# Attention and a feed-forward block in one kernel: twelve weight loads put behind small attention loads in the DMA queue

## The chip, the cores and the metric

The kernel runs on one core of a Trainium2 chip. The metric is the device time of one execution in microseconds (us), as the median of several runs. The core's engines are TensorE (PE in the profile, with its weight loads as PEld), VectorE (DVE), ScalarE (ACT), GpSimd (POOL) and SyncE (SP). SP computes nothing here; it issues nearly all DMAs, one after the other, in one queue.

## The reference

Attention without a score matrix, on 8 batches of 8 heads with 576 tokens and head width 64, and then a feed-forward block with a squared ReLU on the 4608 tokens of width 512, hidden width 2048. All data is float32.

```python
def _attn_ref(q, k, v):
    q_s = np.exp(q - np.max(q, axis=-1, keepdims=True))
    q_s = q_s / (np.sum(q_s, axis=-1, keepdims=True) + 1e-09)
    k_s = np.exp(k - np.max(k, axis=2, keepdims=True))
    k_s = k_s / (np.sum(k_s, axis=2, keepdims=True) + 1e-09)
    kv = np.einsum('bhsd,bhse->bhde', k_s, v)
    return np.einsum('bhsd,bhde->bhse', q_s, kv)

def _moe_ref(x, w_in, w_out):
    r = np.maximum(x @ w_in, 0.0)
    return (r * r) @ w_out
```

## The kernel before

**Feed-forward.** The 4608 tokens are taken in nine blocks of 512: eight blocks with the first 512 tokens of each batch, and a ninth with the 64 left over from each. A block has 16 steps, one for each 128 columns of the hidden width. A step has two halves on TensorE: h (lines 406 to 408, twelve products of 128x512 that multiply `wi[fc]` with the attention's output) and o (lines 440 to 442, twelve products that multiply the squared ReLU with `wo[fc]` and add up in four banks). Float32 precision comes from pairs: x, g and the weights are each kept as a high and a low part, and each product is made three times (high with high, low with high, high with low). The o half of a step runs two steps behind its h half (`LAG`).

**Weights.** The 16 pieces of `w_in` (i0 to i15) and the 16 of `w_out` (o0 to o15), 512 KB each, are loaded once, by `load_w` (lines 147 and 149), as raw tiles that stay in SBUF. In the first block each piece is split once into its high and low part by `split_weight`: ScalarE does lines 164 and 166, VectorE lines 168 and 169 (the two halves of a split on VectorE), ScalarE makes the high part (line 176) and GpSimd the low part (line 177). The scratch bank `bank3` is shared by all splits, so line 166 of the next one waits for line 169 of the one before. `load_more(n)` loads the o piece of step n and the i piece of step n + 4; step n of the first block splits the i piece of step n + 4 and the o piece of step n + 2.

**Attention.** A batch has four pairs of heads. For a pair, VectorE takes the maximum of k (`m`, line 218) and of q (`qm`, line 260); for the second batch TensorE transposes m (line 222) and spreads it (line 250); VectorE subtracts it from k (`ke`, line 255), ScalarE takes the exponential, TensorE multiplies with v (line 299), and VectorE scales the result (`rs`, `kvn`, lines 307 to 315). TensorE then transposes q and multiplies (lines 347 to 358) and the result is stored as high and low parts `x_hi`, `x_lo` (lines 188, 189). The first batch is done at the start. While the feed-forward of one batch runs, the attention of the next one is put in between its steps, by the table `slots`. The k, q and v tiles of the second and later batches have two buffers (`NB`), so pairs 0 and 2 use kt0, qt0 and vt0, and pairs 1 and 3 use kt1, qt1 and vt1. A pair's loads are called for when the pair two before it has reached a given unit (`us[i]`, line 538).

**What sets the order.** The program is written as a sequence, and a scheduler with a simulated timeline orders each engine's instructions from it, with priorities (`tc.high_priority`) and with explicit bounds (`tc.issue_after`). On the chip each engine then runs its list in that order. SP's list works with eight completion semaphores in turn: an issue waits for the landing of the load that was issued eight places earlier, and for the engine that last read the buffer. Behind the second batch's first two pairs, lines 519 to 522 call for all weights that are still missing:

```python
    for pr in range(NB):
        load_pair(1, pr)
    for n in range(AHEAD, NFC):
        load_more(n)
```

With `AHEAD = 4` that is twelve o pieces and eight i pieces. The loads of the second batch's third and fourth pairs (pairs 2 and 3) are called for later, from line 538.

Of the kernel before, what the change touches and what calls it, by code (L numbers as in the profile page):

```python
# [17 lines left out]
HALF = 64  # L18
LOW = 5
HIGH = 4  # L20
# [5 lines left out]
EARLY_SPLITS = [("o",2),("o",3),("i",4),("o",0)]  # L26
OFFSET = 100
AHEAD = 4
EARLY = 8
PRE = 4  # L30
LOADS = "k0 q0 v0 k1 q1 v1 k2 q2 w0 v2 k3 q3 v3 w1 w2 w3".split()
# [11 lines left out]
def attention_ffn_kernel(ctx: ExitStack, tc: tile.TileContext, q, k, v, w_in, w_out, out):  # L43
    nc = tc.nc

    B, H, S, D = q.shape
    DM, DF = w_in.shape
    NPAIR = H // 2
    NCC = DM // P
    NFC = DF // P  # L50
# [19 lines left out]
    NB = 2  # L70
# [46 lines left out]
    def load(dst, src, b, pr, n):  # L117
        s = src[b, 2 * pr : 2 * pr + 2]
        lo = s[:, :SPLIT, :].rearrange("h (p j) d -> p h j d", j=LOW)
        hi = s[:, SPLIT:, :].rearrange("h (p j) d -> p h j d", j=HIGH)  # L120
        if n < 2 or b == 0:
            e = nc.scalar if (b, pr, n) in ACT_LOADS else nc.sync
            e.dma_start(dst[:HALF], lo)  # L123
            e.dma_start(dst[HALF:, :, :HIGH, :], hi)
        else:
            for h in range(2):
                nc.sync.dma_start(dst[:HALF, h, :, :D], lo[:, h])
                nc.sync.dma_start(dst[HALF:, h, :HIGH, :D], hi[:, h])

    def tiles(b, pr):  # L130
        i = pr if b == 0 else pr % NB
# [5 lines left out]
    def load_pair(b, pr):  # L137
        for n in range(3):
            load_one(b, pr, n)

    chunks, last = [], []

    def load_w(part, fc):
        raw = stay.tile([P, 512, 2], U32, name=f"raw_{part}{fc}", tag=f"{part}{fc}")
# [333 lines left out]
    us = [attention(0, pr) for pr in range(NPAIR)]  # L478
# [3 lines left out]
    for c in LOADS:  # L482
        i = int(c[1])
# [6 lines left out]
    def load_more(n):  # L490
        load_w("o", order0[n])
        if n + PRE < NFC:
            load_w("i", order0[n + PRE])
# [24 lines left out]

    for pr in range(NB):
        load_pair(1, pr)  # L520
    for n in range(AHEAD, NFC):
        load_more(n)
    steps = [(0, fc) for fc in order0] + [(blk, fc) for blk in range(1, B + 1) for fc in range(NFC)]
    LAG = 2
# [3 lines left out]
    for b in range(1, B):  # L528
        for pr in range(NPAIR):
            if b == 1:  # L530
                base, offs = FIRST_KV + EARLY_STEP * pr, EARLY_AT
            else:
                base, offs = 2 * NFC * (b - 1) + 1 + STEADY_STEP * pr, STEADY_AT
            us = attention(b, pr)
            nxt = b * NPAIR + pr + NB
            if nxt < B * NPAIR:
                i = 5 if b == 1 else 4
                us[i] = lambda f=us[i], nxt=nxt: (f(), load_pair(nxt // NPAIR, nxt % NPAIR))
            for u, o in zip(us, offs):
                slots.setdefault(base + o, []).append(u)  # L540
    for cc, u in enumerate(left_units()):
        slots.setdefault(2 * NFC * (B - 1) + 4 + 6 * cc, []).append(u)


    def in_slot(i):
        for u in slots.get(i, []):
# [60 lines left out]
```

## Time and profile before

| | us |
|---|---|
| median of 3 runs | 905.96 (905.91 to 908.08) |
| the profiled execution | 906.89 |
| its span, first to last instruction | 905.0 |
| TensorE busy in the span | 875.9 |
| VectorE busy in the span | 580.8 |
| ScalarE busy in the span | 408.1 |
| GpSimd busy in the span | 202.1 |

The span is what the trace shows; the profiled execution's own time is 1.89 us longer, and that execution took 0.93 us more than the median of the runs. The mean granted clock of TensorE over the span is 0.993 of full speed. Busy time is a sum over very different stretches: the attention of the first batch and the splitting of the weights fill the first 150 us or so, and from there on the feed-forward products dominate.

### The profile page before, as it was taken

The numbers are of one execution on the slowest core, as the hardware profiler recorded it, in microseconds if no ns is written. First come the engines' busy times: TensorE is split into PE (matmuls) and PEld (weight loads), VectorE is DVE, ScalarE is ACT, GpSimd is POOL, SyncE is SP. The second block draws the span as 40 slices with busy tenths as digits, with TensorE's granted clock in tenths as the row PEclk, the third lists the DMA queues.
The fourth block names the chain that finished last, engine by engine and source line by source line (L and its number), as shares of the span: only waits on it lengthen the run. The fifth ranks groups of instructions, "written<-read, shape, count | busy, mean of one in ns | idle before, by whom it ended". The sixth has DMA issues, their size and how long they took to land.

```text
span 905.0 us, 12673 instructions
## 1 busy us (share of the span) xinstructions
PE 875.9 (97%) x4368; PEld 702.4 (78%) x4368; DVE 580.8 (64%) x1177; ACT 408.1 (45%) x801; POOL 202.1 (22%) x177
## 2 busy tenths in 40 slices
PE   4898989999999999999999999999999999999997
PEld 3576767888878888888888888888888888888885
DVE  6767887887778776878688768876764342222222
ACT  3766756545445443454454444444444232222222
POOL 3666635222213210222122212222222000000000
PEclk9989999999999999999999999999999999999999
DMA  9898211422142223322322123222311030002001
GB/s 234 274 324 246 62 35 54 114 77 82 46 117 71 78 64 89 97 72 71 86 80 81 54 76 96 76 65 65 97 31 32 3 93 1 1 1 46 1 1 46
DMA packets 95743, 73.18 MB, mean 81 GB/s; under 512 B 47552, under 2 KB 85440, under 8 KB 95680
## 3 DMA queue, kind: packets, MB, share of 16 engines
q1 hardware_dynamic: 94944, 71.53, 28.7%
q10 hardware_dynamic: 736, 0.85, 0.4%
q8 instruction: 34, 0.56, 0.2%
q14 instruction: 29, 0.24, 0.1%
HBM read 54.00 MB, written 18.35 MB: 80 GB/s over the span
## 4 chain that ended last, share of the span: by engine, by line
PE 85%; DMA 7%; DVE 4%; SPq 2%; issue 1%; ACT 0%; DVEq 0%
PE bank L406 14%; PE o_ps L440 14%; PE bank L407 14%; PE bank L408 14%; PE o_ps L441 14%; PE o_ps L442 13%; DMA qt<-in_q_dram 4%; DMA raw_i<-in_moe_w_in_dram 3%; PE bank L299 2%; PE bank L378 1%; DMA kt<-in_k_dram 1%; DVE w L169 1%; SPq L149 1%; DVE m L237 1%; SPq L123 0%
## 5 line engine op out<-in xcount | busy, mean ns | idle before, releaser
L406 PE MATMUL bank<-x_hi,wi 128*128 128x512 f32 x568 | 227.6, 401 | 4.3 <-ACT x_hi L188 2.2
L440 PE MATMUL o_ps<-wo,g_hi 128*128 128x512 f32 x576 | 227.5, 397 | 0.8 <-ACT g_hi L419 0.8
L441 PE MATMUL o_ps<-wo,g_hi 128*128 128x512 f32 x576 | 225.7, 392 | 0.0
L407 PE MATMUL bank<-x_lo,wi 128*128 128x512 f32 x568 | 225.6, 397 | 0.0
L408 PE MATMUL bank<-x_hi,wi 128*128 128x512 f32 x568 | 225.2, 396 | 0.0
L442 PE MATMUL o_ps<-wo,g_lo 128*128 128x512 f32 x576 | 224.1, 391 | 0.0
L418 DVE TENSOR_TENSOR r<-r 128x512 f32<-128x512 f32 x128 | 112.0, 875 | 123.3 <-ACT r L412 123.0
L423 DVE TENSOR_TENSOR g_lo<-r,g_hi 128x512 fp32r<-128x512 f32 x132 | 99.3, 752 | 105.8 <-ACT g_hi L419 104.1
L419 ACT CAST g_hi<-r 128x512 fp32r<-128x512 f32 x144 | 89.2, 620 | 129.1 <-PE o_ps L441 77.2
L412 ACT ACTIVATE r<-bank 128x512 f32<-128x512 f32 x142 | 84.5, 596 | 106.1 <-PE bank L408 103.4
L406 PEld LDWEIGHTS bank<-x_hi,wi 128*128 128x128 f32 x568 | 107.6, 190 | 30.9 <-ACT x_hi L188 3.6
L440 PEld LDWEIGHTS o_ps<-wo,g_hi 128*128 128x128 f32 x576 | 108.1, 188 | 25.7 <-ACT g_hi L419 1.0
L408 PEld LDWEIGHTS bank<-x_hi,wi 128*128 128x128 f32 x568 | 107.7, 190 | 24.3
L442 PEld LDWEIGHTS o_ps<-wo,g_lo 128*128 128x128 f32 x576 | 108.1, 188 | 22.9
L441 PEld LDWEIGHTS o_ps<-wo,g_hi 128*128 128x128 f32 x576 | 108.1, 188 | 22.9 <-POOL wo L177 0.2
L407 PEld LDWEIGHTS bank<-x_lo,wi 128*128 128x128 f32 x568 | 107.5, 189 | 22.8 <-issue 0.2
L389 POOL TENSOR_TENSOR x_lo<-xf,x_hi 128x256 fp32r<-128x256 f32 x48 | 39.5, 823 | 378.2 <-ACT x_hi L388 377.4
L332 POOL TENSOR_TENSOR qs<-qT,qs 64x640 fp32r<-64x640 f32 x48 | 81.7, 1703 | 58.7 <-ACT qs L331 50.9
L218 DVE TENSOR_REDUCE m<-kt 128x128 f32<-128x640 f32 x32 | 41.4, 1296 | 18.3 <-DMA kt<-in_k_dram 18.3
L331 ACT CAST qs<-qT 64x640 fp32r<-64x640 f32 x48 | 34.8, 726 | 37.9 <-DMA qT<-bounce 37.4
L380 ACT COPY xf<-bank 64x320 f32<-64x320 f32 (+1 forms) x96 | 37.9, 395 | 22.5 <-PE bank L378 14.3
L265 ACT ACTIVATE qn<-qn 128x640 f32<-128x640 f32 x32 | 23.6, 739 | 53.8 <-DVE qn L262 44.9
(118 smaller groups left out, 775.8 us busy)
## 6 DMA issues: line engine op xcount, KB each, us to landing
out_dram<-o SPq DMA_DIRECT2D x70, 128.0 KB, 2.4
raw_i<-in_moe_w_in_dram SPq DMA_DIRECT2D x16, 512.0 KB, 9.3
raw_o<-in_moe_w_out_dram SPq DMA_DIRECT2D x16, 512.0 KB, 9.0
bounce<-tb SPq DMA_DIRECT2D x24, 320.0 KB, 2.2
qT<-bounce SPq DMA_DIRECT2D x96, 80.0 KB, 2.3
kt<-in_k_dram SPq DMA_DIRECT2D x32, 160.0 KB, 3.0
qt<-in_q_dram SPq DMA_DIRECT2D x30, 160.0 KB, 3.0
vt<-in_v_dram SPq DMA_DIRECT2D x56, 80.0 KB, 2.5
```

The lines of the kernel that those rows point to most:

```text
L218: nc.vector.tensor_reduce(m, kk.rearrange("p h j d -> p h d j"), axis=AX.X, op=ALU.max)
L332: nc.gpsimd.tensor_tensor(qs[other], qT[own], qs[own].bitcast(F32), op=ALU.subtract)
L406: nc.tensor.matmul(ps, wi[fc][:, 0, sl], xh[:, cc, :], start=(cc == 0), stop=False)
L407: nc.tensor.matmul(ps, wi[fc][:, 0, sl], xl[:, cc, :], start=False, stop=False)
L408: last.append(nc.tensor.matmul(ps, wi[fc][:, 1, sl], xh[:, cc, :], start=False, stop=(cc == NCC - 1)))
L412: nc.scalar.activation(r, ps, AF.Relu)
L418: nc.vector.tensor_tensor(r, r, r, op=ALU.mult)
L419: gh = nc.scalar.copy(g_hi, r)
L423: e.tensor_tensor(g_lo, r, g_hi.bitcast(F32), op=ALU.subtract)
L440: nc.tensor.matmul(acc[t], g_hi[:, ts], wo[fc][:, 0], start=(n == 0), stop=False)
L441: nc.tensor.matmul(acc[t], g_hi[:, ts], wo[fc][:, 1], start=False, stop=False)
L442: prev = nc.tensor.matmul(acc[t], g_lo[:, ts], wo[fc][:, 0], start=False, stop=(n == NFC - 1))
```

## The change

Only the first four of the missing steps (n = 4 to 7: o4 to o7 and i8 to i11) are still called for at the old place. The weights of n = 8 to 11 (o8 to o11, i12 to i15) are called for right after the loads of the second batch's pair 2, and those of n = 12 to 15 (o12 to o15) right after the loads of its pair 3, each under `tc.issue_after` with the last v load of that pair, so that they can't be put ahead of it.

```diff
--- before.py
+++ after.py
@@ -26,6 +26,8 @@
 EARLY_SPLITS = [("o",2),("o",3),("i",4),("o",0)]
 OFFSET = 100
 AHEAD = 4
+
+LATER = 8, 12, 16
 EARLY = 8
 PRE = 4
 LOADS = "k0 q0 v0 k1 q1 v1 k2 q2 w0 v2 k3 q3 v3 w1 w2 w3".split()
@@ -125,7 +127,7 @@
         else:
             for h in range(2):
                 nc.sync.dma_start(dst[:HALF, h, :, :D], lo[:, h])
-                nc.sync.dma_start(dst[HALF:, h, :HIGH, :D], hi[:, h])
+                dmas.append(nc.sync.dma_start(dst[HALF:, h, :HIGH, :D], hi[:, h]))
 
     def tiles(b, pr):
         i = pr if b == 0 else pr % NB
@@ -138,7 +140,7 @@
         for n in range(3):
             load_one(b, pr, n)
 
-    chunks, last = [], []
+    chunks, last, dmas = [], [], []
 
     def load_w(part, fc):
         raw = stay.tile([P, 512, 2], U32, name=f"raw_{part}{fc}", tag=f"{part}{fc}")
@@ -518,7 +520,7 @@
 
     for pr in range(NB):
         load_pair(1, pr)
-    for n in range(AHEAD, NFC):
+    for n in range(AHEAD, LATER[0]):
         load_more(n)
     steps = [(0, fc) for fc in order0] + [(blk, fc) for blk in range(1, B + 1) for fc in range(NFC)]
     LAG = 2
@@ -535,12 +537,20 @@
             nxt = b * NPAIR + pr + NB
             if nxt < B * NPAIR:
                 i = 5 if b == 1 else 4
-                us[i] = lambda f=us[i], nxt=nxt: (f(), load_pair(nxt // NPAIR, nxt % NPAIR))
+                us[i] = lambda f=us[i], nxt=nxt: (f(), load_next(nxt))
             for u, o in zip(us, offs):
                 slots.setdefault(base + o, []).append(u)
     for cc, u in enumerate(left_units()):
         slots.setdefault(2 * NFC * (B - 1) + 4 + 6 * cc, []).append(u)
 
+
+    def load_next(nxt):
+        load_pair(nxt // NPAIR, nxt % NPAIR)
+        i = nxt - NPAIR - NB
+        if i + 1 < len(LATER):
+            with tc.issue_after(dmas[-1].ins):
+                for n in range(LATER[i], LATER[i + 1]):
+                    load_more(n)
 
     def in_slot(i):
         for u in slots.get(i, []):
```

In the listings of the built programs, lines of the changed kernel stand two higher than those of the kernel before. In SP's queue twenty weights stood in a row before. This is its last part, from the thirteenth weight on (qt0 is q of the second batch's pair 2; q of pair 3, qt1, and k of pair 2, kt0, come right behind these rows):

```order
L149 DMA raw_o10_594<-in_moe_w_out_dram 128x1024
L123 DMA qt0_82<-in_q_dram 64x2x320
L147 DMA raw_i14_596<-in_moe_w_in_dram 128x4x256
L124 DMA qt0_82<-in_q_dram 64x2x256
L367 DMA x_left_77<-left_499 128x64
L367 DMA x_left_77<-left_541 128x64
L149 DMA raw_o11_598<-in_moe_w_out_dram 128x1024
L147 DMA raw_i15_600<-in_moe_w_in_dram 128x4x256
L149 DMA raw_o12_602<-in_moe_w_out_dram 128x1024
L149 DMA raw_o13_604<-in_moe_w_out_dram 128x1024
L149 DMA raw_o14_606<-in_moe_w_out_dram 128x1024
L149 DMA raw_o15_608<-in_moe_w_out_dram 128x1024
```

This stands there now, from the eighth weight on:

```order
L149 DMA raw_i11_584<-in_moe_w_in_dram 128x4x256
L125 DMA qt0_82<-in_q_dram 64x2x320
L126 DMA qt0_82<-in_q_dram 64x2x256
L369 DMA x_left_77<-left_499 128x64
L369 DMA x_left_77<-left_541 128x64
L125 DMA qt1_83<-in_q_dram 64x2x320
L126 DMA qt1_83<-in_q_dram 64x2x256
L125 DMA kt0_78<-in_k_dram 64x2x320
L126 DMA kt0_78<-in_k_dram 64x2x256
L130 DMA vt0_80<-in_v_dram 64x4x64
L129 DMA vt0_80<-in_v_dram 64x5x64 x2
L130 DMA vt0_80<-in_v_dram 64x4x64
```

The q loads of pairs 2 and 3 and the k load of pair 2 now come right behind the eighth weight; o8 and the seven weights after it stand behind the v loads of pair 2. The last four weights come to stand behind the v loads of pair 3, right ahead of the next batch's first q and k loads:

```order
L130 DMA vt1_81<-in_v_dram 64x4x64
L129 DMA vt1_81<-in_v_dram 64x5x64 x2
L130 DMA vt1_81<-in_v_dram 64x4x64
L151 DMA raw_o12_933<-in_moe_w_out_dram 128x1024
L151 DMA raw_o13_935<-in_moe_w_out_dram 128x1024
L151 DMA raw_o14_937<-in_moe_w_out_dram 128x1024
L151 DMA raw_o15_939<-in_moe_w_out_dram 128x1024
L125 DMA qt1_83<-in_q_dram 64x2x320
L125 DMA kt0_78<-in_k_dram 64x2x320
L126 DMA kt0_78<-in_k_dram 64x2x256
L126 DMA qt1_83<-in_q_dram 64x2x256
```

Before, no weight stood there: o12 to o15 were rows of the first listing.

On VectorE two places matter. The first is after the split of o1, where `kvn0` of the second batch's pair 0 is made. Before:

```order
L169 SCALAR_TENSOR_TENSOR w_630<-raw_o1_176,bank3_89 128x512
L307 TENSOR_SCALAR rs_743<-bank0_86 128x1
L308 RECIPROCAL rs_743<-rs_743 128x1
L315 TENSOR_SCALAR kvn0_84<-bank0_86,rs_743 64x64 x2
L168 SCALAR_TENSOR_TENSOR bank3_89<-bank3_89,raw_i6_174 128x512
L224 TENSOR_REDUCE mc_801<-bank0_86 128x1
L169 SCALAR_TENSOR_TENSOR w_657<-raw_i6_174,bank3_89 128x512
L416 TENSOR_TENSOR r_773<-r_773,bank1_87 128x512
L168 SCALAR_TENSOR_TENSOR bank3_89<-bank3_89,raw_o4_570 128x512
L169 SCALAR_TENSOR_TENSOR w_663<-raw_o4_570,bank3_89 128x512
```

Now:

```order
L171 SCALAR_TENSOR_TENSOR w_606<-raw_o1_176,bank3_89 128x512
L262 TENSOR_REDUCE qm_941<-qt0_82 128x10
L309 TENSOR_SCALAR rs_719<-bank0_86 128x1
L310 RECIPROCAL rs_719<-rs_719 128x1
L262 TENSOR_REDUCE qm_1103<-qt1_83 128x10
L317 TENSOR_SCALAR kvn0_84<-bank0_86,rs_719 64x64 x2
L220 TENSOR_REDUCE m_960<-kt0_78 128x128
L170 SCALAR_TENSOR_TENSOR bank3_89<-bank3_89,raw_i6_174 128x512
L226 TENSOR_REDUCE mc_793<-bank0_86 128x1
L418 TENSOR_TENSOR r_765<-r_765,bank1_87 128x512
L171 SCALAR_TENSOR_TENSOR w_633<-raw_i6_174,bank3_89 128x512
L170 SCALAR_TENSOR_TENSOR bank3_89<-bank3_89,raw_o4_570 128x512
```

The q maxima of pairs 2 and 3 and the k maximum of pair 2 (`m_960<-kt0`) have moved ahead of the split of i6; before, they were rows 97, 113 and 115 of VectorE's list, where the rows above are 86 to 95. In the same way the k maximum of pair 3 and the q maximum of the third batch's pair 0 have moved ahead of `kvn1` of pair 1.

The second place is around the split of i13, which h of step 13 needs; `r_1314` is the squared ReLU of step 12. Before, the whole split stood in front:

```order
L168 SCALAR_TENSOR_TENSOR bank3_89<-bank3_89,raw_i13_592 128x512
L240 TENSOR_REDUCE m5_1530<-m4_1525 32x4
L308 RECIPROCAL rs_1275<-rs_1275 128x1
L240 TENSOR_REDUCE m5_1530<-m4_1525 32x4 x3
L169 SCALAR_TENSOR_TENSOR w_1127<-raw_i13_592,bank3_89 128x512
L315 TENSOR_SCALAR kvn1_85<-bank2_88,rs_1275 64x64 x2
L244 COPY mt_1521<-m5_1530 128x128
L245 STREAM_TRANSPOSE mb_1535<-mt_1521 128x128
L232 STREAM_TRANSPOSE mt_1740<-m_1738 128x128
```

and `r_1314` followed in row 187, behind the whole split of o11. Now:

```order
L239 COPY m4_1744<-m1_1742 32x4 x4
L242 TENSOR_REDUCE m5_1749<-m4_1744 32x4 x4
L170 SCALAR_TENSOR_TENSOR bank3_89<-bank3_89,raw_i13_738 128x512
L246 COPY mt_1740<-m5_1749 128x128
L418 TENSOR_TENSOR r_1314<-r_1314,bank1_87 128x512
L171 SCALAR_TENSOR_TENSOR w_1127<-raw_i13_738,bank3_89 128x512
L170 SCALAR_TENSOR_TENSOR bank3_89<-bank3_89,raw_o11_744 128x512
L171 SCALAR_TENSOR_TENSOR w_1133<-raw_o11_744,bank3_89 128x512
L425 TENSOR_TENSOR g_lo_1317<-r_1314,g_hi_1316 128x512
```

Now line 171 of i13 and the whole split of o11 come behind the squared ReLU of step 12. The other splits from i9 on have moved back against the attention's and the feed-forward's rows in the same manner. TensorE's order is the same as before up to h of step 13.

## Rows read from the trace of the kernel before

**Rows 1.** Part 1 of the page: busy time of each engine, its share of the span, and its instructions.

```profile
PE 875.9 (97%) x4368; PEld 702.4 (78%) x4368; DVE 580.8 (64%) x1177; ACT 408.1 (45%) x801; POOL 202.1 (22%) x177
```

**Rows 2.** The waits of TensorE over the whole span: the waiting instruction, what released it, then microseconds in total, times, and the longest one.

```profile
PE bank L222 <- DVE m L218: 3.3, 1, 3.3
```

**Rows 3.** TensorE's timeline: start in us, duration in us, engine, line, operation, tile written and tiles read, size, count; in brackets the idle time before it, where there was some, and what ended it.

```profile
43.76 0.74 PE L406 MATMUL bank<-x_hi,wi 128*128 128x512 f32 x2 [2.22 <-ACT x_hi L188]
...
46.21 0.69 PE L358 MATMUL bank<-qT,kvn 128*128 128x64 f32 x2 [1.25 <-DVE x_lo L189]
...
82.18 0.27 PE L349 MATMUL bank<-ident,qn 64*128 64x64 f32 x1
...
85.77 0.33 PE L222 MATMUL bank<-ident,m 128*128 128x128 f32 x1 [3.32 <-DVE m L218]
...
105.51 0.33 PE L222 MATMUL bank<-ident,m 128*128 128x128 f32 x1 [0.78 <-ACT kvn L313]
...
120.76 0.87 PE L299 MATMUL bank<-vt,ke 128*64 128x65 f32 x20 [0.69 <-DVE x_lo L189]
...
124.53 0.27 PE L349 MATMUL bank<-ident,qn 64*128 64x64 f32 x1
...
133.14 0.51 PE L406 MATMUL bank<-x_hi,wi 128*128 128x512 f32 x1 [1.17 <-DVE r L416]
```

**Rows 4.** Windows, with the busy time of each engine in a stretch: start and end, length, then PE, PEld, DVE, ACT and POOL with the instructions in brackets, the granted clock of TensorE, the busy share of the DMA engines, and GB/s.

```profile
46.00:48.00 2.00, 1.79 (x5) 1.59 (x6) 2.00 (x4) 1.09 (x4) 1.16 (x1) 0.50 0.72 180
60.00:82.00 22.00, 22.00 (x131) 16.93 (x129) 14.71 (x30) 17.37 (x34) 15.51 (x13) 1.00 1.07 326
84.00:86.00 2.00, 0.23 (x2) 0.23 (x3) 1.71 (x2) 1.16 (x2) 1.48 (x2) 1.00 0.62 170
86.00:88.00 2.00, 2.00 (x7) 1.57 (x7) 1.86 (x3) 0.00 (x0) 0.60 (x1) 0.54 0.63 173
88.00:90.00 2.00, 2.00 (x7) 1.59 (x6) 2.00 (x4) 1.16 (x2) 0.00 (x0) 0.61 0.53 119
100.00:110.00 10.00, 9.02 (x59) 6.61 (x57) 9.63 (x25) 7.19 (x17) 4.68 (x4) 1.00 0.25 64
130.00:140.00 10.00, 8.83 (x38) 6.55 (x37) 9.51 (x19) 5.80 (x11) 3.88 (x3) 1.00 0.03 12
```

**Rows 5.** SP's timeline: start in us and duration of an issue, and the load that it issues.

```profile
45.97 0.59 SPq L149 DMA_DIRECT2D raw_o<-in_moe_w_out_dram  x1
...
73.16 0.60 SPq L124 DMA_DIRECT2D qt<-in_q_dram  x1
```

**Rows 6.** The chain of work that ended last, in order of time: start, microseconds, and what the chain stood on. For a DMA that is from its issue to its landing.

```profile
50.92 9.82 DMA raw_i<-in_moe_w_in_dram
60.76 11.31 DMA qt<-in_q_dram
...
73.16 9.88 DMA qt<-in_q_dram
...
93.61 2.82 DMA kt<-in_k_dram
```

**Rows 7.** VectorE's timeline, with the columns of group 3.

```profile
60.48 0.69 DVE L169 SCALAR_TENSOR_TENSOR w<-raw_o,bank 128x512 uint32<-128x512 uint32 x1
62.27 0.16 DVE L307 TENSOR_SCALAR rs<-bank 128x1 f32<-128x1 f32 x1 [1.10 <-PE bank L299]
...
66.50 0.68 DVE L416 TENSOR_TENSOR r<-r,bank 128x512 f32<-128x512 f32 x1
...
72.16 0.82 DVE L260 TENSOR_REDUCE qm<-qt 128x10 f32<-128x640 f32 x1 [2.23 <-DMA qt<-in_q_dram]
...
81.12 0.58 DVE L315 TENSOR_SCALAR kvn<-bank,rs 64x64 f32<-64x64 f32 x2
...
83.13 0.82 DVE L260 TENSOR_REDUCE qm<-qt 128x10 f32<-128x640 f32 x1 [0.70 <-DMA qt<-in_q_dram]
...
84.46 1.25 DVE L218 TENSOR_REDUCE m<-kt 128x128 f32<-128x640 f32 x1
...
91.14 0.82 DVE L255 TENSOR_TENSOR ke<-kt,bank 128x640 f32<-128x640 f32 x1 [0.93 <-PE bank L250]
...
96.52 1.31 DVE L218 TENSOR_REDUCE m<-kt 128x128 f32<-128x640 f32 x1 [1.12 <-DMA kt<-in_k_dram]
...
99.95 0.69 DVE L168 SCALAR_TENSOR_TENSOR bank<-bank,raw_o 128x512 uint32<-128x512 uint32 x1
...
114.81 0.82 DVE L260 TENSOR_REDUCE qm<-qt 128x10 f32<-128x640 f32 x1 [1.63 <-DMA qt<-in_q_dram]
...
126.46 0.69 DVE L169 SCALAR_TENSOR_TENSOR w<-raw_i,bank 128x512 uint32<-128x512 uint32 x1
...
132.40 0.69 DVE L416 TENSOR_TENSOR r<-r,bank 128x512 f32<-128x512 f32 x1
```

**Rows 8.** Timelines of GpSimd (POOL) and ScalarE (ACT), with the columns of group 3.

```profile
90.97 1.26 POOL L262 TENSOR_TENSOR qn<-qt,qm 128x640 f32<-128x640 f32 x1 [4.37 <-PE bank L347]
...
127.18 0.63 ACT L166 ACTIVATE bank<-raw_o 128x512 f32<-128x512 f32 x1 [0.53 <-DVE w L169]
127.76 0.60 ACT L176 CAST wi<-w 128x512 fp32r<-128x512 f32 x1
...
128.44 1.29 POOL L177 TENSOR_TENSOR wi<-w,wi 128x512 fp32r<-128x512 f32 x1 [1.62 <-ACT wi L176]
```

## The prediction

> **What bounds the kernel now.** I read the page first: TensorE is busy 97% of the span and VectorE 64% [rows 1], so time can only come out of the places where TensorE stands still. The waits of TensorE by releaser show the longest one after the start: 3.3 us before the max transpose of line 222, released by VectorE's k maximum of line 218 [rows 2]. TensorE's timeline places it: the last transpose ends about 82.4, the next instruction starts at 85.77 with 3.32 us idle before it [rows 3]. The windows show what follows: the granted clock is 1.00 until 86, then 0.54 and 0.61 in the two slices to 90 [rows 4]. [...]
>
> Why was it late? I write B1.p and B2.p for pair p of the second and the third batch, h_k and o_k for the two halves of a feed-forward step. VectorE did qm of B1.3 at 83.13 after waiting for its q load, and only then m of B1.2, at 84.46 [rows 7]. That q load was issued at 73.16 and landed 9.88 us later; the q of B1.2, issued at 60.76, took 11.31 us [rows 5, 6], where the k load issued at 93.61 with no weights ahead took 2.82 us [rows 6]. All stand in SP's queue behind the twenty 512 KB weight loads that begin at 45.97 [rows 5].
>
> From 100 to 140 another engine decides: VectorE is busy 9.63 and 9.51 of 10 us, TensorE 9.02 and 8.83 [rows 4], and the waits left on TensorE (0.78, 0.73, 0.69, 1.17) [rows 3] all end with VectorE or with what hangs on it. After 140 TensorE is full. What counts is therefore when TensorE gets h_13 going, at 133.14 [rows 3], and a microsecond saved before that is saved only if VectorE is early too.
>
> **The change part by part.** No instruction is added or dropped. Two things move: the loads in SP's queue, and, because the scheduler then counts on weights that come later, VectorE's instructions.
>
> *Loads.* Eight weights stay in front, and the eighth, issued at 50.92, landed 9.82 us later, at 60.7 [rows 6]. A load is issued when the one eight places earlier has landed, so the last of the six small loads now behind these weights, k of B1.2, is issued at about 60.8 and lands 2.8 us later, by the row of 93.61 [rows 6]: 63.6. The two q loads land near 62. VectorE ends its o_1 split at 61.1 and now has qm of B1.2, the two small kv rows (62.27), qm of B1.3, kvn0 and m of B1.2 in front of the i_6 split [rows 7]. With 0.82 for a qm and 1.25 for the m, m runs 64.1 to 65.3 and r of h_4 ends at 66.9, against 67.2 before (66.50 + 0.68). These fill VectorE's own wait of 1.10 and its later wait of 2.23 for q [rows 7]; nothing is lost. The next eight weights follow the v loads of B1.2, from about 64, and at the spacing before (the eighth landed at 60.7 after a first issue at 45.97, 1.85 us each at most) [rows 5, 6] the last lands at 79 or sooner; VectorE took the first of them, o_8, at 99.95 and i_13 at 126.46 [rows 7]. Weights are nowhere late. The last four follow the v loads of B1.3.
>
> *The stall.* The m of B1.2 is ready 17 us before TensorE asks for it, so the 3.3 us go. But three rows now stand ahead of kvn1 (m of B1.3, qm of B2.0, a half split of i_8), and one half split no longer does: 1.25 + 0.82 + 0.69 - 0.69 by the busy times, about 1.9 as neighbours overlap. kvn1 ended at 81.7 (81.12 + 0.58) [rows 7] and now ends at 83.6. It reads the bank that h_7 writes, so TensorE waits 1.2 us there. That leaves ke of B1.2 at about 87.7, against 91.14 [rows 7]: 3.4 us early.
>
> *VectorE from there to h_13.* ke of B1.2 frees the k tile for B2.0. Its load is issued behind the q load of B2.1, which waits for GpSimd's qn of B1.3. That now follows the low part of i_8, whose split ends near 84.4: 84.4 + 0.6 + 0.6 on ScalarE + 1.29 + 1.26 on GpSimd is 88.1 [rows 8]. So the second half of the k load goes out at 89.4 and lands at 92.2. VectorE waits for it longer than before, but m of B2.0 starts at 92.2 instead of 96.52 [rows 7]: 4.3 us early. From that m to the end of r of h_12 VectorE took 96.52 to 133.1, 36.6 us, with one wait of 1.63 for q [rows 7]. In the new order the i_13 split ends behind r of h_12, not before it; the stretch to its end holds one half split more (+0.69) and one row more to cover the q wait (-0.7), so it stays near 36.5 and ends at 128.7. Now the new term: h_13 must wait for i_13. Before, that split ended at 127.15 (126.46 + 0.69), six microseconds before use [rows 7]. After it ScalarE does line 166 of the next weight and the high part (0.63, 0.60), then GpSimd the low part, 1.29 [rows 8], which the third product of h_13 needs: 128.7 + 0.55 + 0.55 + 1.3 = 131.1. Taking off the two products that run before it, h_13 starts in effect at 130.6, against 133.14: **2.5 us early, not 5.**
>
> *Clock.* TensorE's own lead is larger: r of h_11 and i_12 come some 5 us early, so h_12 starts near 120 instead of right behind 124.53, and h_13 is reached 7.2 us later (124.8 to 131.97, which is 133.14 less the wait of 1.17) [rows 3], near 127. TensorE so stands some 3.4 us before h_13 and inside it. The one wait of that size in the trace, 3.32 us, was followed by the lower level [rows 3, 4], and so was the pair 2.22 and 1.25 near 44, after which the window from 46 to 48 shows 0.50; single waits up to 1.17 were not [rows 3, 4]. I take the fall: 1.7 us given back. [...]
>
> *Sum.* Gain 2.5 - 1.7 = 0.8 us. The profiled execution took 906.89 (span 905.0), so 906.1; the median of the runs, 905.96, lies 0.93 below that execution: **905.2 us**. Bounds of what is unknown: the wait before h_13 without a fall gives 903.5. If VectorE bound nothing any more, the whole 5.0 would stay, 901.0. Behind h_13 the splits of i_15 and o_13 also come later in the new order, with about half a microsecond to spare by the same rows; if each loses what the wait before h_13 lost in the trace (1.17), 907.5. I take the middle case because the two stretches 100 to 110 and 130 to 140, where VectorE has under 0.5 us of 10 left, are the nearest evidence.
>
> **The rivals.**
>
> *Full gain.* The stall and the low clock go and VectorE keeps up: 5.0 us, 901.0. For it: VectorE was busy only 14.7 of the 22 us from 60 to 82 [rows 4] and gets three rows done there early. Against it: the same order puts three half splits behind ke of B1.2, where VectorE has no room. Chance 0.20.
>
> *Slower: the k load of B2.0 behind the last four weights.* Before, no weight stood ahead of it (2.82 us). Now o_12 to o_15 do, issued after the v loads of B1.3, about 82 to 84. At up to 1.85 us each they land by about 90, and the k load is the next thing that VectorE wants, with nothing to do meanwhile. If it waits as the q at 73.16 did (9.88), it lands 7.1 us later, the whole chain to h_13 slips, and with the fall of the clock the sum is 2.5 - 7.1 - 1.7 = -6.3: 912.3. It decides from about 3.5 us of delay (0.8 + 2.7), where the result leaves the band of no change: 908.7. For it: SP's queue showed this wait twice. Against it: four weights are 2 MB, not 10. [...] Chance 0.15.
>
> *The stall comes back at the same place.* k of B1.3 and q of B2.0 now stand behind the second eight weights; they should land near 79, and VectorE reads them from about 80, ahead of kvn1. Two to three microseconds late, h_7 waits as line 222 did, and the result is no change, 905 to 907. Chance 0.08.
>
> The change might not have come out as written, but the order listings show it in SP's queue and on VectorE; no chance is kept for that.
>
> **How the numbers follow.** The forecast keeps 0.57: 905.2, with its own range 903.5 to 907.5. A difference below 0.3% (2.7 us) can't be told from none here. Same: 0.57 less 0.05 at its lower and 0.02 at its upper edge, plus 0.08, is 0.58. Faster: 0.20 + 0.05 = 0.25. Slower: 0.15 + 0.02 = 0.17. The range runs from the full gain, 901.0, to the point just past where the slow rival begins to show, 909.0; it leaves out the far part of that rival and gains beyond 5 us.
>
> **What would show it.** Right: no wait above 1.5 us between 80 and 90 and a full clock there; a wait of about 1.2 us before h_7; m of B2.0 near 92; the longest wait of TensorE after 50 now before h_13 or between its products, ended by ScalarE's or GpSimd's part of i_13, with a lower clock behind it. Wrong: h_13 starting near 128 without a wait (full gain), m of B2.0 after 95 (the weights ahead of k), or a wait before line 222 or line 250 between 64 and 70, which would say that the early q and k rows hold VectorE.

## The result, and the profile after

The changed kernel takes 912.13 us (median of 6 runs, 909.16 to 914.62) against 906.11 of the kernel before in the same runs: a ratio of 1.0064, 95% interval 1.0044 to 1.0084. It is slower by 6.0 us, where 905.2 was forecast. The profiled execution took 914.62 (span 912.8), the slowest of the six, so its trace shows about 2.5 us more loss than the median. The six executions differ in TensorE's mean granted clock, from 0.996 in the fastest down to 0.988 in the slowest (0.993 in the profiled execution before), so much of their spread is time at the lower clock.

The answer to [rows 1] is part 1 of the page:

```profile
PE 879.3 (96%) x4368; PEld 704.8 (77%) x4368; DVE 584.5 (64%) x1177; ACT 407.6 (45%) x801; POOL 201.1 (22%) x177
```

The work is the same; TensorE is busy 3.4 us longer, which the windows below put down to the lower clock, and stands still 4.4 us longer. TensorE's timeline, as in [rows 3], says where:

```profile
86.22 0.76 PE L408 MATMUL bank<-x_hi,wi 128*128 128x512 f32 x1 [3.10 <-DVE kvn L317]
...
103.73 0.50 PE L408 MATMUL bank<-x_hi,wi 128*128 128x512 f32 x1 [0.51 <-DVE r L418]
...
110.35 0.47 PE L224 MATMUL bank<-ident,m 128*128 128x128 f32 x1 [3.36 <-ACT kvn L315]
...
127.23 0.87 PE L301 MATMUL bank<-vt,ke 128*64 128x65 f32 x20 [0.88 <-DVE x_lo L191]
...
139.32 0.49 PE L408 MATMUL bank<-x_hi,wi 128*128 128x512 f32 x1 [1.02 <-ACT wi L178]
...
140.68 0.50 PE L410 MATMUL bank<-x_hi,wi 128*128 128x512 f32 x1 [0.64 <-POOL wi L179]
...
160.06 1.19 PE L442 MATMUL o_ps<-wo,g_hi 128*128 128x512 f32 x4 [0.82 <-ACT wo L178]
```

The wait of 3.32 before line 222 is gone. Two of its size have come: 3.10 before h_7, which waits for kvn1, and 3.36 before the transposition of m of B1.3, which waits for the kvn of B1.2 on ScalarE. The windows, as in [rows 4], show that TensorE came out of both at the lower clock:

```profile
84.00:86.00 2.00, 0.00 (x0) 0.00 (x0) 1.99 (x6) 0.32 (x2) 0.50 (x1) 0.85 0.71 180
86.00:88.00 2.00, 1.78 (x4) 1.49 (x5) 1.24 (x4) 0.85 (x2) 0.00 (x0) 0.50 0.96 381
88.00:90.00 2.00, 2.00 (x6) 1.54 (x5) 1.20 (x2) 0.32 (x1) 1.28 (x1) 0.50 1.01 406
90.00:92.00 2.00, 2.00 (x7) 1.50 (x7) 0.00 (x0) 0.23 (x1) 0.00 (x0) 0.50 0.29 117
...
110.00:112.00 2.00, 1.65 (x5) 1.36 (x6) 1.66 (x4) 1.90 (x5) 1.13 (x1) 0.50 0.25 68
112.00:114.00 2.00, 2.00 (x6) 1.56 (x5) 1.27 (x3) 1.00 (x2) 1.28 (x1) 0.50 0.29 83
114.00:116.00 2.00, 2.00 (x7) 1.46 (x6) 0.53 (x1) 0.44 (x1) 0.00 (x0) 0.50 0.00 0
```

**The first stall.** VectorE's timeline, as in [rows 7]:

```profile
65.25 1.31 DVE L220 TENSOR_REDUCE m<-kt 128x128 f32<-128x640 f32 x1
...
82.90 1.29 DVE L220 TENSOR_REDUCE m<-kt 128x128 f32<-128x640 f32 x1 [2.46 <-DMA kt<-in_k_dram]
...
84.19 0.79 DVE L262 TENSOR_REDUCE qm<-qt 128x10 f32<-128x640 f32 x1
84.91 0.68 DVE L170 SCALAR_TENSOR_TENSOR bank<-bank,raw_i 128x512 uint32<-128x512 uint32 x1
85.51 0.57 DVE L317 TENSOR_SCALAR kvn<-bank,rs 64x64 f32<-64x64 f32 x2
...
93.01 0.81 DVE L257 TENSOR_TENSOR ke<-kt,bank 128x640 f32<-128x640 f32 x1
...
98.75 1.32 DVE L220 TENSOR_REDUCE m<-kt 128x128 f32<-128x640 f32 x1 [2.80 <-DMA kt<-in_k_dram]
```

m of B1.2 is done by 66.6 (forecast 65.3). But m of B1.3 waited until 82.90 for its k, and kvn1 is the fourth row behind it. The chain, as in [rows 6], has the two k loads:

```profile
72.40 10.41 DMA kt<-in_k_dram
...
95.20 3.47 DMA kt<-in_k_dram
```

The first, of B1.3, was issued right behind the second eight weights and took 10.41 us. SP's timeline has the first and the last of these weights; the last took 12.6 us to land, at 82.2:

```profile
65.23 0.59 SPq L151 DMA_DIRECT2D raw_o<-in_moe_w_out_dram  x1
...
69.56 0.55 SPq L149 DMA_DIRECT2D raw_i<-in_moe_w_in_dram  x1
```

The other load, of B2.0, took 3.47 us: the last four weights, which it stands behind, had landed (by 91.7). It was late because it was issued late. The load ahead of it in the queue, q of B2.1, waited for the row of GpSimd that reads the q loaded there before, and that row for TensorE, which was at half clock (granted 0.50 from 86 to 92, in the windows above):

```profile
92.54 1.26 POOL L264 TENSOR_TENSOR qn<-qt,qm 128x640 f32<-128x640 f32 x1 [2.86 <-PE bank L349]
```

**The second stall.** Three rows of GpSimd's timeline, a row of VectorE's, and then pieces of the chain that ended last, around 104 (start, microseconds, engine, tile, line):

```profile
101.00 1.26 POOL L277 TENSOR_TENSOR qn<-qn,qs 128x640 f32<-128x640 f32 x1 [1.54 <-DVE qs L276]
103.67 1.30 POOL L179 TENSOR_TENSOR wo<-w,wo 128x512 fp32r<-128x512 f32 x1 [1.41 <-ACT wo L178]
104.92 1.30 POOL L425 TENSOR_TENSOR g_lo<-r,g_hi 128x512 fp32r<-128x512 f32 x1
```

```profile
103.59 2.83 DVE L239 COPY m<-m 32x4 f32<-32x4 f32 x4
```

```profile
103.67 0.06 DVE m L239
...
103.75 1.24 DVE m L239
...
105.00 1.24 DVE m L239
...
106.25 0.17 DVE m L239
```

The timelines of VectorE and ScalarE behind them:

```profile
107.82 0.16 DVE L309 TENSOR_SCALAR rs<-bank 128x1 f32<-128x1 f32 x1
...
109.68 0.62 ACT L315 ACTIVATE kvn<-bank,rs 64x64 f32<-64x64 f32 x2
```

Two of the four 32x4 copies (line 239) last 1.24 us each: the first starts as GpSimd's split of 103.67 runs and ends with it, the second starts beside the instruction of 104.92 and ends with that. The other two take some 0.15 and 0.17 (the first began at 103.59; the 0.06 is only its piece of the chain). The row rs of B1.2 and its reciprocal stand behind the copies on VectorE. The two kvn wait for them on ScalarE, where they also stand behind line 168 and a high part, which wait for the half split of VectorE that comes after the copies. TensorE's transposition, which writes the bank that kvn reads, starts at 110.35.

### The profile page after: what moved, and what is told of

It is laid out like the page before. It is cut to its first block, busy times and chain, and to the rows that moved or that the text cites. A ratio compares the mean times of both kernels' runs of the same rounds, so it can differ in the third digit from the quotient of the medians.

```text
span 912.8 us, 12674 instructions
## 1 busy us (share of the span) xinstructions
PE 879.3 (96%) x4368; PEld 704.8 (77%) x4368; DVE 584.5 (64%) x1177; ACT 407.6 (45%) x801; POOL 201.1 (22%) x177
## 4 chain that ended last, share of the span: by engine, by line
PE 85%; DVE 4%; DMA 4%; issue 3%; ACT 1%; POOL 1%; SPq 1%; DVEq 0%; POOLq 0%; ACTq 0%
PE o_ps L442 14%; PE o_ps L443 13%; PE bank L408 13%; PE o_ps L444 13%; PE bank L410 13%; PE bank L409 13%; PE bank L301 2%; DMA kt<-in_k_dram 2%; DMA qt<-in_q_dram 2%; PE bank L380 1%; DVE m L220 1%; DVE bank L170 1%; DVE qm L262 1%; SPq L125 0%; DVE w L171 0%
## 5 line engine op out<-in xcount | busy, mean ns | idle before, releaser
L420 DVE TENSOR_TENSOR r<-r 128x512 f32<-128x512 f32 x128 | 108.8, 850 | 118.5 <-ACT r L414 118.1
L425 DVE TENSOR_TENSOR g_lo<-r,g_hi 128x512 fp32r<-128x512 f32 x132 | 101.6, 770 | 108.7 <-ACT g_hi L421 107.3
L333 ACT CAST qs<-qT 64x640 fp32r<-64x640 f32 x48 | 34.9, 726 | 37.8 <-DMA qT<-bounce 37.3
L383 DVE TENSOR_TENSOR xf<-bank,xf 64x320 f32<-64x320 f32 (+1 forms) x96 | 42.7, 445 | 5.1 <-ACT xf L382 2.9
```

Of the source, the lines that this page charges most:

```text
L420: nc.vector.tensor_tensor(r, r, r, op=ALU.mult)
L425: e.tensor_tensor(g_lo, r, g_hi.bitcast(F32), op=ALU.subtract)
```

## The experiments

To change one row and nothing else, each engine's list was fixed row by row and then edited; a "-" is where a row stood and a "+" where it stands now. The kernel before with fixed lists and one row moved (the fifth experiment below) takes the time of the kernel before, so fixing costs nothing that shows. The changed kernel with fixed lists and no other edit was not run; "less than the changed kernel" below is less than the 912.13 of its six executions, whose ratio has the interval 1.0044 to 1.0084. Each run's ratio is to the kernel before on the same chip (906.3 to 906.5 there).

**1. The late k, ahead of the weights.** SP's list:

```
  vt (B1.2), four rows
+ kt (B1.3), two rows
+ qt (B2.0), two rows
  raw_o8, raw_i12, raw_o9, raw_i13, raw_o10, raw_i14, raw_o11, raw_i15
- kt (B1.3), two rows
- qt (B2.0), two rows
```

> The changed kernel with its orders kept, but in the DMA queue the k of B1.3 and the q of B2.0 stand ahead of the second eight weights instead of behind them. Theory Q (the landing of that k is what is late): it lands near 76 us instead of 82.8, VectorE's reduction of it starts by 80.5 and not at 82.90, kvn1 ends near 83.6, h_7 waits 1.0 to 1.5 us instead of 3.1, TensorE's clock falls less; 2 to 4 us less than the changed kernel, 908 to 910. Rival V (the rows that VectorE now has ahead of kvn1 are the cost, whenever the data come): h_7 waits over 2.5 us, within 1 us of the changed kernel, 911 to 913. Both: the wait of 3.4 us near 110 stays.

It took 913.48 us, ratio 1.0082 (1.0069 to 1.0096): no gain. But the first stall went as theory Q had it: m of B1.3 starts at 81.20 without a wait, kvn1 at 83.82, and h_7 waits 0.58. What took its place stands in TensorE's timeline and the chain of this run:

```profile
84.54 0.47 PE L408 MATMUL bank<-x_hi,wi 128*128 128x512 f32 x1 [0.58 <-ACT raw_i L166]
102.18 1.42 PE L301 MATMUL bank<-vt,ke 128*64 128x65 f32 x20 [4.53 <-DVE x_lo L191]
```

```profile
91.68 6.90 DMA kt<-in_k_dram
```

Here the last four weights went out at 86.20 to 90.2 and the k of B2.0 right behind them; it took 6.90 us, VectorE waited for it, and x_lo stands behind that row. This is the prediction's slower rival, in a kernel other than the one it was made for. Neither expectation had it.

**2. That rival by itself.** As 1, and the last four weights behind the loads that follow them:

```
  vt (B1.3), four rows
- raw_o12, raw_o13, raw_o14, raw_o15
  qt (B2.1), kt (B2.0), kt (B2.0), qt (B2.1)
+ raw_o12, raw_o13, raw_o14, raw_o15
```

> The run with the k of B1.3 ahead of the second eight weights, and in the DMA queue the last four weights behind the k and q of B2.0 and B2.1 instead of ahead of them. Theory L (there the k of B2.0 was late, 98.67, behind the last four weights, as the prediction's slower rival had it for the change itself): it lands by 95.5, VectorE waits for it under 4 us instead of 6.8, the wait of 4.5 us for x_lo near 102 falls under 1.0; 3 to 5 us less than that run, 908 to 910; the wait behind the slow copies stays over 2. Rival (x_lo is late for another reason): that wait stays over 3, 912 to 914.

908.32 us, ratio 1.0027 (1.0017 to 1.0037), 5.2 less than run 1: m of B2.0 starts at 94.15 and the wait for x_lo falls from 4.53 to 0.16. Theory L holds. The wait of 3.36 behind the copies stays. So both places of the weights in the queue matter, and in run 1 what was gained at one was lost at the other.

**3. VectorE's order at the first stall.** SP's queue as in the changed kernel; on VectorE:

```
  rs (B1.1)
- m<-kt (B1.3)
  reciprocal of rs
- qm<-qt (B2.0)
- half split of i_8
  kvn1, two rows
+ half split of i_8
  mc (B1.2), half split of i_8
+ m<-kt (B1.3)
+ qm<-qt (B2.0)
```

> The changed kernel with its DMA queue kept; on VectorE alone the reductions of the k of B1.3 and of the q of B2.0 stand behind kvn1 instead of ahead of it. Theory Q with V (the late k costs only because kvn1 stands behind it): kvn1 ends near 81.7, h_7 waits under 0.3 us, the reduction still waits for its k until 82.9, which nobody on TensorE waits for; 4 to 5 us less than the changed kernel, 907 to 908. Rival Q alone (the crowded queue is late for TensorE too, through v or ke): a wait of over 2 us comes back within 5 us behind h_7, 911 to 912.

909.32 us, ratio 1.0028 (1.0017 to 1.0038): 2.8 less than the changed kernel, where 4 to 5 was expected. Two rows of VectorE:

```profile
80.43 0.58 DVE L317 TENSOR_SCALAR kvn<-bank,rs 64x64 f32<-64x64 f32 x2
...
83.72 1.33 DVE L220 TENSOR_REDUCE m<-kt 128x128 f32<-128x640 f32 x1
```

TensorE has no wait from 58 to 95, and then 1.11 us for x_lo, up to 97.01. The k is as late as before, and nobody on TensorE waits for it: what made the late load cost anything is that kvn1 stood behind it. The second stall is now the only one of its size:

```profile
105.03 0.48 PE L224 MATMUL bank<-ident,m 128*128 128x128 f32 x1 [3.36 <-ACT kvn L315]
```

**4. The second stall, twice.** First rs of B1.2 and its reciprocal, and on ScalarE the two kvn, moved up (the expectation calls this rs B1.3, but it is the kvn of B1.2 that reads it):

```
  VectorE                            ScalarE
  r                                + kvn (B1.2), two rows
+ rs (B1.2), reciprocal              line 168 of the split of o_8
  four copies (B2.0)                 high part of i_10
  ...                              - kvn (B1.2), two rows
- rs (B1.2)
- reciprocal
```

> The changed kernel, but the sums rs of B1.3 and their reciprocals stand ahead of the four copies of B2.0 on VectorE, and the two kvn of ScalarE ahead of the split that stands before them. Theory C (the second stall is rs and kvn behind copies that take 2.83 us): the wait of 3.36 us near 110 falls under 0.6 us, TensorE keeps its clock from 110 to 116, the copies still take over 2 us; 4 to 5 us less than the changed kernel, 907 to 908; the wait of h_7 at 86 stays 3.1. Rival (the transposition waits for something else that is as late, such as the split of ScalarE or the m of B2.0): a wait of over 2 us stays there, 911 to 913.

910.02 us, ratio 1.0039 (1.0026 to 1.0051), 2.1 less. The transposition runs at 104.91 without a wait, but a wait of 2.21 for r came at 110.18, with the lower clock behind it (0.50 from 112 to 114): the copies still take 2.73 us, and the splits and r behind them are late all the same. Theory C was half of it; the copies themselves were left as the delay. So the second time only they were moved, ahead of the row r:

```
- r
  four copies (B2.0)
+ r
```

> The changed kernel with one row of VectorE moved: the four 32x4 copies of B2.0 stand ahead of the product r (the square of h) and not behind it, so that they run from about 103.1 us, before GpSimd starts its split at 103.67. Theory G (a copy waits for the GpSimd instruction that runs beside it): the four take 0.6 to 1.0 us instead of 2.83, rs and kvn come 1 to 2 us earlier, the wait near 110 falls from 3.4 to 1 to 2 us, the r that now stands behind them costs TensorE 0.5; 1 to 2 us less than the changed kernel, 910 to 911.5. Rival (the copies are slow by themselves): they still take over 2.5 us, r is late by as much, 913 to 915.

909.37 us, ratio 1.0045 (1.0031 to 1.0059), 2.8 less. VectorE's and GpSimd's timelines and TensorE's row:

```profile
101.58 0.67 DVE L239 COPY m<-m 32x4 f32<-32x4 f32 x4
```

```profile
99.46 1.26 POOL L277 TENSOR_TENSOR qn<-qn,qs 128x640 f32<-128x640 f32 x1 [0.94 <-DVE qs L276]
102.14 1.27 POOL L179 TENSOR_TENSOR wo<-w,wo 128x512 fp32r<-128x512 f32 x1 [1.41 <-ACT wo L178]
```

```profile
106.80 0.33 PE L224 MATMUL bank<-ident,m 128*128 128x128 f32 x1 [0.51 <-ACT kvn L315]
```

Between GpSimd's instructions, the same four copies take 0.67 us instead of 2.83. Theory G holds. The gain of 2.8 is more than it expected, but in both kernels of 4 the interval overlaps that of the changed kernel; these gains are read from the rows, and the time settles them only in 6.

**5. The loads alone, the order alone, and both.** First the changed kernel's queue (its first 112 rows) with the four other engines in the kernel before's order, row by row. (TensorE's list had changed too, and not only behind h of step 13, as was said ahead of the prediction: a few products inside o_6 and o_10 are swapped.)

> The loads alone: the changed kernel's DMA queue up to its third group of weights, and on the four other engines the kernel before's order, instruction by instruction. Theory V (the stall before the transposition of m of B1.2 was made by VectorE's order more than by the load: of 3.3 us the load gives the 0.7 for which qm waited): that wait falls to 2.4 to 2.8 us, h_7 waits for nothing, the wait of 3.4 near 110 is not there; 904.5 to 906. Rival P (as the prediction had it, the late loads make the stall): the wait is under 1 us, 900 to 902. Rival Q alone (the moved loads are themselves the harm): 909 or more.

905.32 us, ratio 0.9986 (0.9978 to 0.9995): 1.1 less than before. The early loads take 3.32 to 2.23 and no more, since m stands behind kvn1, qm and a half split. So the moved loads by themselves do no harm; they do it only together with the order of the engines that the scheduler made for them. TensorE's row:

```profile
82.89 0.47 PE L224 MATMUL bank<-ident,m 128*128 128x128 f32 x1 [2.23 <-DVE m L220]
```

Then the kernel before, with m of B1.2 moved up and its own queue:

```
  kvn1, two rows
+ m<-kt (B1.2)
  half split of o_6
  qm<-qt (B1.3)
  half split of o_6
- m<-kt (B1.2)
```

> The kernel before, its DMA queue kept, with one row of VectorE moved: the reduction m of the k of B1.2 stands right behind kvn1, ahead of a split and of the qm that waited for its q until 83.13. No weight is moved. Theory V with Q (order and load are both needed: the k of B1.2 lands there only about when that q does, 82 to 84): the wait before the transposition falls from 3.3 to between 1.3 and 2.3 us, 904.5 to 906 us. Rival V alone (the order was the whole cost): it falls under 0.6 us, 901 to 903. Rival Q alone (the load is the whole cost): the wait stays over 2.8, no change.

906.04 us, ratio 1.0001 (0.9992 to 1.0009), no change: the row waits for its k until 83.25, and TensorE for the row, 3.15 us. Its rival Q holds. Then both, m of B1.2 behind x_lo and the early loads:

```
  x_lo
+ m<-kt (B1.2)
  qs
  ...
  half split of o_6
- m<-kt (B1.2)
```

> The loads alone with the orders of the kernel before, and one row of VectorE moved: the reduction m of the k of B1.2 stands behind the x_lo near 72 us, where its data have long come, and not behind kvn1 and qm. Theory V (the early load is worth the whole stall only if VectorE takes the reduction up early): the wait of 2.2 us before the transposition near 83 falls under 0.4 and TensorE keeps its clock there; 3 to 4.5 us less than the loads alone, 901 to 902.5. Rival (the row that moves up makes kvn1, a split or the qs of B1.2 late, and TensorE waits for that): a wait of 1.5 us or more stands within 10 us of the old one, 904 to 906.

904.55 us, ratio 0.9983 (0.9974 to 0.9992). The stall and the lower clock are gone (the clock is 1.00 from 60 to 170); 1.06 before line 360 and 0.45 for x_lo came in their place. The gain on the loads alone is 0.8 us by the medians, with intervals that overlap, and not 3 to 4.5: theory V is right about the wait and wrong about its worth.

**6. Are the two stalls all of it?** Both moves on VectorE, of 3 and of the second part of 4:

> The changed kernel with both moves on VectorE at once: kvn1 ahead of the late reduction, and the four copies ahead of r. If the two stalls are two separate losses, their gains add (2.8 and 2.8 us of the changed kernel's 912.1): 905.5 to 907.5, no wait over 1.3 us left between 80 and 112, full clock from 60 to 112. Rival (they are one delay that the second stall takes over): 908 or more, with a wait of over 2 us left in that stretch.

906.56 us, ratio 1.0002 (0.9992 to 1.0012): the gain is 5.6, as if the two of 2.8 add, and with both moves the change costs nothing. It does not gain either. Waits of 1.59 for x_lo and 1.34 for r were left near 98 (the expectation allowed 1.3), with the lower clock behind them (0.50 from 100 to 102). For the rest, behind 112, the other engines were put in the kernel before's order from there on:

> Both moves on VectorE, and behind the stretch of the two stalls (from the ke of B2.0 on VectorE and ScalarE, from the transposition of m of B1.3 on TensorE) all engines in the kernel before's order. Theory S (the changed kernel's later splits are a third loss: two waits of 1.0 and 0.6 us at h_13 and one of 0.8 to 1.1 before o near 155, against one of 1.2 before): 1 to 2 us less than both moves alone, 904 to 906. Rival (these waits are taken back later): within 0.5 us of both moves alone.

913.49 us, ratio 1.0073 (1.0058 to 1.0088). It does not answer the question: it lost 4.55 us near 203, where queue and engines followed different orders. With the queue, too, in the kernel before's order behind row 112:

> The run before it lost 4.55 us near 203, where its DMA queue still went by the changed kernel's order and the engines by the kernel before's; here the queue too goes by the kernel before's order behind its first 112 rows. Theory S (the changed kernel's later splits are a third loss, waits of 3.0 us in all between 125 and 160 against 1.5): no wait over 2 us behind 112, and 1 to 2 us less than both moves alone, 904.5 to 906. Rival (taken back later, or the seam costs as much): within 0.5 us of both moves alone, 906 to 907.

905.79 us, ratio 1.0001 (0.9991 to 1.0011), against 906.56 and 1.0002. The waits between 112 and 170 fell from 4.1 to 2.5 us, but at the seam a wait of 1.81 came. Whether the changed kernel's later splits are a third loss stays undecided: the time can't tell the two.

**7. The fastest version.** Loads alone with m moved up, and three more rows (this qT is that of B1.1 and this rs that of B1.2; the expectation counts both one pair too high):

```
  ScalarE                            VectorE
+ qT (B1.1)                        - qm<-qt (B2.1)
  line 168 of the split of o_7       mt, x_lo
  high part of i_9                 + qm<-qt (B2.1)
  r                                  ...
- qT (B1.1)                        + rs (B1.2), reciprocal
                                     four copies (B2.0)
                                   - rs (B1.2), reciprocal
```

> The loads alone with m of B1.2 moved up, and three more rows moved: on ScalarE the copy of qT of B1.2 ahead of the split that stands before it, on VectorE the qm of B2.1 behind x_lo, and rs of B1.3 with its reciprocals ahead of the four copies. Theory W (what that kernel lost again after its stall went are the waits of 1.06 for qT, 0.45 for x_lo and 0.77 for kvn): these three fall under 0.3 us each and it is 1 to 2.3 us faster than without them, 902 to 903.5. Rival (the chains behind take it back: r, x_lo and the waits near 114 to 130 grow by as much): 904 to 905.

904.09 us, ratio 0.9977 (0.9968 to 0.9987), the lowest of all, 2.2 less than before. Its interval overlaps that of the run without the three rows, 904.55. Against that run it is the rival that holds: x_lo fell to 0.18 and kvn to nothing, but the wait for r grew from 0.51 to 1.23, 0.63 came behind it, and line 360 still waits 1.07.

**The books.** For the profiled execution of each kernel but the one that lost its time near 203, from 58 to 170: the idle times of TensorE that the timeline shows, added up, and the work lost to the lower clock, which is busy time times (1 - granted clock) in windows of 1 us.

| run | waits | lower clock | sum | median, and before's beside it |
|---|---|---|---|---|
| before | 6.9 | 1.7 | 8.6 | 906.1 |
| the change | 11.2 | 5.9 | 17.1 | 912.1, 906.1 |
| 1, k first | 12.5 | 1.6 | 14.1 | 913.5, 906.5 |
| 2, last weights later | 8.5 | 1.7 | 10.2 | 908.3, 906.3 |
| 3, kvn1 first | 8.8 | 2.7 | 11.5 | 909.3, 906.5 |
| 4, rs first | 9.8 | 3.4 | 13.2 | 910.0, 906.5 |
| 4, copies first | 8.7 | 1.7 | 10.4 | 909.4, 906.3 |
| 6, both | 7.0 | 1.7 | 8.7 | 906.6, 906.3 |
| 6, both, order and queue of before behind | 8.2 | 0 | 8.2 | 905.8, 906.4 |
| 5, loads alone | 5.9 | 1.6 | 7.5 | 905.3, 906.5 |
| 5, m up alone | 7.0 | 2.9 | 9.9 | 906.0, 906.3 |
| 5, loads and m up | 5.3 | 0 | 5.3 | 904.6, 906.3 |
| 7 | 5.7 | 0 | 5.7 | 904.1, 906.3 |

Against the row of before, the difference in the sum is the difference in the time within 1.6 us, but for the change's own row. That one overshoots (8.5 more, where the median lost 6.0), since its profiled execution was the slowest: by the two profiled executions' own times, 914.62 and 906.89, it lost 7.7.

## Why the prediction was wrong

*Loads.* The early q and k loads did what was said: m of B1.2 ran 65.25 to 66.56 (forecast 64.1 to 65.3), and VectorE's own waits took it up. **The step that failed is the sentence on the next eight weights: "at the spacing before ... the last lands at 79 or sooner".** They went out from 65.23, not from about 64; the last was issued at 69.56 and landed 12.6 us later, at 82.2, and the k of B1.3 behind it at 82.81. From 65.23 that is 2.1 us a weight, not "1.85 us each at most". The bound was taken from eight weights with only more weights right behind them, and was called an upper one without a reason. The runs point at the k and q loads that stand right behind here: with them ahead (runs 1 and 2) the same eight weights took 15.1 and 15.7 us in all, 1.9 and 2.0 each; with them behind, 16.1 to 17.1 in the changed kernel and in five runs with its queue there (3, both of 4, the loads alone, 6). No run was made to test it. "Weights are nowhere late" was true of the weights, and the wrong question; the small loads behind them were late.

*The stall.* The rows ahead of kvn1 were counted rightly. With the k there in time (runs 1 and 2) kvn1 starts at 83.8 to 84.1 and h_7 waits 0.58, against an end of kvn1 at 83.6 and a wait of 1.2 in the forecast. With it 3.8 us later than forecast, kvn1 ended at 86.08 and the wait was 3.10. The third rival names this place and this mechanism; it had 0.08, because the landing was worked out once and not given a range.

*VectorE up to m of B2.0.* Forecast 92.2, measured 98.75. GpSimd's qn of B1.3 ended at 93.80 instead of 88.1, behind TensorE, which came out of the stall at half clock (0.50). Where the stall is taken away (run 3), m starts at 93.41: the working was right, its start was not. The prediction named "m of B2.0 after 95" as the sign of weights ahead of that k; the sign came, from another cause.

*From there to h_13.* **The second step that failed** is the sentence "From that m to the end of r of h_12 VectorE took 96.52 to 133.1, 36.6 us", which moved a stretch as a block and kept it near 36.5 to the end of the split of i_13. It took 39.3 (98.75 to 138.07):

```profile
137.39 0.68 DVE L171 SCALAR_TENSOR_TENSOR w<-raw_i,bank 128x512 uint32<-128x512 uint32 x1
```

Run 3, which has the same second stall and half clock, has 39.4; with the copies moved between GpSimd's instructions the same stretch took 35.0 (second kernel of 4) and 36.3 (the first of 6). Run 2 and the first kernel of 4 lie between, at 37.3 and 36.6. The block's rows did not keep their price here when what runs beside them moved. GpSimd's two instructions moved against the copies, and 1.77 us became 2.83, with rs behind four rows more (three reductions and a half split). The trace of before had the sign: one copy took 1.26 us beside GpSimd's instruction of 102.20 to 103.49, where the median of all is 0.157. VectorE's timeline, the chain and GpSimd's timeline before:

```profile
101.93 1.77 DVE L237 COPY m<-m 32x4 f32<-32x4 f32 x4
```

```profile
102.26 1.26 DVE m L237
```

```profile
102.20 1.29 POOL L423 TENSOR_TENSOR g_lo<-r,g_hi 128x512 fp32r<-128x512 f32 x1 [1.04 <-ACT g_hi L419]
```

This is the second stall, 3.36 us and a second stretch at half clock; no case of the prediction had it, and it is why the third rival's "no change, 905 to 907" was too good.

*h_13 and the clock.* The wait of 3.4 us before h_13 was oversized: 1.02 and 0.64, without a lower clock (1.00 from 138 to 146), and 1.00 and 0.63 in run 6, where TensorE was not late. It replaced a wait of 1.17 [rows 3], so this term costs some 0.5. The 1.7 that the forecast gives back for the clock is 2 x (1 - 0.54) + 2 x (1 - 0.61) by the windows of [rows 4], and with the wait of 3.3 it makes the 5.0; the books have 1.7 for the kernel before, too, and 5.9 for the change, in its two stretches at half clock.

*The premise.* "The m of B1.2 is ready 17 us before TensorE asks for it, so the 3.3 us go" held here only because the scheduler had moved the row of VectorE, too. The load gave 1.1 of the 3.3 us (run 5), the order alone nothing. The full gain of 5.0 did not come even with both: the stall went, and waits of 0.5 to 1.1 on the chains of qT, x_lo and r came out from behind it. That is what the prediction said of the stretch from 100 to 140, and it kept 0.57 for a middle case. The slower rival's 912.3 is near the result by chance: its k of B2.0 behind four weights was not late here (3.47 us). The mechanism is real where the loads come earlier (run 1).

## What to carry to other kernels

A load that moves in a queue can make late what stands behind its new place (here a k took 10.41 us behind eight weights, where one with no weights ahead took 2.82 [rows 6]): work out that landing with a range, and then look in the reader's list for what stands behind the waiting row, since there it turned into a stall (3.10 us). A stretch of rows that moved on one engine did not keep its duration when another engine's rows moved against it (39.3 us, where 36.6 was taken over from before); look for rows whose longest is several times their median (1.26 us against 0.157). A stall that hides other chains is worth less than its length: here removing 3.3 us and its half-clock stretch gave 1.7 to 2.2. And where a scheduler orders the engines by the loads, a moved load moves them all: here the loads alone gained 1.1 us, and with the new order they lost 6.0.

## What was not expected of the hardware

**Copies on VectorE that ended with GpSimd's instruction.** A 32x4 float32 copy took 0.157 us in the median of the 96 in the kernel before. The two of 1.24 us in the changed kernel and the one of 1.26 in the kernel before began while an instruction of GpSimd ran, and ended within 0.03 us of its end; moved between GpSimd's instructions, four took 0.67 instead of 2.83. It was not only copies: in the second kernel of 4, line 264 took 1.71 us beside GpSimd's instruction of 110.47 to 111.77, and 0.81 at 138.84, where VectorE started first (GpSimd's next began at 139.41). What holds these rows up, no run shows.

```profile
110.74 1.71 DVE L264 TENSOR_TENSOR qn<-qt,qm 128x640 f32<-128x640 f32 x1
```

```profile
110.47 1.30 POOL L425 TENSOR_TENSOR g_lo<-r,g_hi 128x512 fp32r<-128x512 f32 x1 [0.32 <-PE bank L349]
```

**The same wait brought the lower clock in one run and not in another.** Windows of run 3 and then of run 2, which both had a wait of 3.36 us, up to 105.03 and up to 106.04:

```profile
105.00:107.00 2.00, 1.97 (x5) 1.60 (x6) 1.66 (x4) 1.92 (x4) 0.80 (x1) 0.50 0.38 103
107.00:109.00 2.00, 2.00 (x6) 1.60 (x5) 1.27 (x3) 0.67 (x2) 1.28 (x1) 0.50 0.15 49
```

```profile
106.00:108.00 2.00, 1.96 (x9) 1.65 (x10) 1.69 (x4) 1.96 (x5) 0.82 (x1) 1.00 0.34 97
...
134.00:136.00 2.00, 1.92 (x6) 1.52 (x7) 1.85 (x3) 1.30 (x3) 1.21 (x2) 0.76 0.00 0
136.00:138.00 2.00, 2.00 (x7) 1.58 (x6) 1.48 (x3) 0.00 (x0) 0.11 (x1) 0.50 0.00 0
```

Run 3 goes on at half clock (granted 0.50 from 105 to 109) for some 5 us; run 2 goes on at 1.00, and falls later (0.50 from 136 to 138), behind waits of 1.00 and 0.64. Run 3 passes waits of 1.02 and 0.65 there without a fall (1.00 from 134 to 138). The prediction took a wait of this size to bring the fall, from the one of 3.32 before [rows 3, 4]; what decides it, no run shows. A stretch at half clock cost 1.6 to 3.0 us here (1.6 in run 1, 3.0 and 2.9 in the change).
